# Routed rows added by an indirect gather and an indirect write in place of one-hot products, beside an exchanged front end

## The chip, the cores and the metric

The kernel runs on one core of a Trainium2 chip. A core has five engines with a queue of instructions each: TensorE (PE: matrix products; its weight loads are listed apart as PEld), VectorE (DVE), ScalarE (ACT), GpSimd (POOL) and SyncE (SP), which here only issues transfers. Sixteen DMA engines move data between HBM and the on-chip memories. Transfers can be issued from SP, ACT or GpSimd. The metric is the device time of one execution in microseconds, the median of several runs. The profile is one execution of the same program; its span (116.4 us) is the time between the first and last event of the core and is a little shorter than the device time.

## The reference, cut to what matters

Input x has 2048 tokens of 640 columns. The output is x plus a linear attention block plus a block that routes: it picks the eight tokens with the highest router score, runs them through a gated MLP, and adds the result to these eight rows only.

```python
xn = _layernorm(x)                                   # (1, 2048, 640)

# A: linear attention, 32 heads of 20 columns
q, k, v = split(xn @ wqkv)
phi = lambda t: jnp.where(t > 0, t + 1, jnp.exp(t)) + 1e-6
kv = einsum("bhsd,bhse->bhde", phi(k), v);  z = einsum("bhsd->bhd", phi(k))
A = ((phi(q) @ kv) / (phi(q) . z + 1e-6)) @ wo

# B: eight routed tokens
r = xn @ w_r
idx = argsort(-r)[:, :8]
y = (silu(x_sel @ w_gate) * (x_sel @ w_up)) @ w_down # x_sel: the 8 rows of xn
y = y * sigmoid(r_sel)
B = xn + scatter_add(zero, idx, y)                   # y lands in 8 of 2048 rows

out = x + A + B
```

## The kernel before: the parts that matter

The 2048 tokens are 16 tiles of 128 (T = 16, P = 128); D = 640 and KC = D / P = 5. The program fixes the order on each engine by the order of the calls. It has three stages:

1. For each tile t: layernorm, a transpose of the normalised tile (xnT), the keys K, phi of the keys (PHa on ACT, PHb on DVE), and G, which sums phi(k)-transposed times xn over all tiles.
2. The queries, kv, the folded matrix Mb = kv x wo, the denominators, and the routed MLP, woven together.
3. Output: for each tile phi(q) x Mb, plus the routed rows, plus x + xn, and a store.

Layernorm of one tile goes through small steps:

```python
def ln_a(t):   # statistics of the first 320 columns, DVE (ln_b: the others)
    dve.bn_stats(out=sts[t][:, 0, :], in_=XX[:, t, 1, 0:320])
def ln_g(t):   # mean and variance
    dve.bn_aggr(out=MV[:, t, :], in_=sts[t][:])
def ln_s(t):   # variance + eps on DVE, square root by a power on GpSimd
    dve.tensor_scalar(out=t2[:], in0=MV[:, t, 1:2], scalar1=EPS_BF16, ...)
    pool.tensor_tensor(out=ss[t][:], in0=t2[:], in1=halfc[:], op=ALU.pow)
def ln_c(t, eng):   # c = mean - x, on ACT or DVE
def ln_xn(t, ...):  # SR = 1 / s, xn = -c * SR  -> XX[:, t, 0, :], DVE
```

In the front end before, tiles 0 and 1 are only centred ahead of their transpose (`CT = 2`); the factor 1/sigma goes into the scale of the exponential and the relu. The tiles up to 5 are transposed on TensorE with copies on ACT, those from tile 6 (`TD = 6`) by DMA.

```python
def wk_ld(k0, k1):
    ld(act, wk[:, k0:k1, 0:D], wqkv_v[:, k0:k1, D : 2 * D])
ld(sp, XX[:, 0, 1, :], x_v[:, 0, :])
wk_ld(0, 3)
ld(sp, XX[:, 1, 1, :], x_v[:, 1, :])
wk_ld(3, KC)
ld(sp, XX[:, 2, 1, :], x_v[:, 2, :])
ld(act, wr[:], ...)
act.preload_act_table_set("natural_log_exp_and_others")
# ... cut ...
def PHa(t, hs=(0, 1)):
    kw = {"scale": SR[:, t : t + 1]} if t < CT else {}
    for h in hs:
        act.activation(ek[:, sl], src, AF.Exp, **kw)
        act.activation(rk[:, sl], src, AF.Relu, **kw)
# ... cut ...
stats(0); ln_c0(0, ((0, 3 * P), (3 * P, D))); ln_s(0)
tr_now(0, 0, 5)                 # transpose of the centred tile 0
stats(1); ln_c0(1); ln_s(1); ln_r(0)
K(0, (0, 1), range(0, 2))
tr_now(1, 1, 2)
# ... cut ...
K(0, (0, 1), range(2, KC))
# ... cut: tiles 2 to 5, then the regular loop ...
for t in range(TD, T):
    K(t); PHa(t); rcopy(t)
    # ... PHb(t - 1), ln_xn(t + 2), tr_dma(t + 2), statistics of t + 3 and t + 4 ...
    if t >= 14:
        logit(t - 14, dve)      # router scores of tiles 0 and 1, by DVE
    G(t - 1)
```

The routed rows. `cols[:, 0]` holds the eight token numbers and `cols[:, 1]` their gates, repeated in each group of 32 partitions; `ysb` holds the eight gated MLP rows in the same layout. `onehot()` turns a table of token numbers into OH, which is 1 where a column's token is that of the partition's row. In the output stage a product of OH and ysb starts the sum of every tile, whether or not a routed token lies in it:

```python
def out_sc(ts):                 # two tiles, two halves each: four products
    for t in ts:
        b = obank(t)
        for h in range(2):
            g = 2 * (t % 2) + h
            pe.matmul(PS[:, b + h, 0:HW], lhsT=OH[32 * g : 32 * g + 8, t * P : (t + 1) * P],
                      rhs=ysb[32 * g : 32 * g + 8, h * HW : (h + 1) * HW], start=True, stop=False)
def out_mm(t):                  # ten products of 128 x 320
    for h in range(2):
        for kc in range(KC):
            pe.matmul(PS[:, b + h, 0:HW], lhsT=pqT[:, kc, t * P : (t + 1) * P],
                      rhs=Mb[:, kc, h * HW : (h + 1) * HW], start=False, ...)
def out_ev(t):                  # the last tile goes out in three parts, through DVE and ACT
    dve.tensor_tensor(out=ot, in0=PS[:, b : b + 2, 0:HW], in1=XX[:, t, 1, :], op=ALU.add)
    ld(sp, out_v[:, t, :], ot[:])
# ... cut ...
for t in range(6, T):
    if t % 2 == 0:
        out_sc((t, t + 1))
    out_one(t)                  # out_mm(t), out_ev(t)
```

Three, and from tile 8 on four, pairs of PSUM banks take the output tiles by turns, and four buffers the outgoing rows.

Of the kernel before, what the change touches and what calls it, by code (L numbers as in the profile page):

```python
# [22 lines left out]
CT = 2  # L23
TD = 6
FQ = F // 4
EPS_BF16 = 1.0013580322265625e-05
LOW = S - 1

# [9 lines left out]
def kernel(  # L38
# [62 lines left out]
    def ld(eng, dst, src):  # L101
        eng.dma_start(dst, src)

    def wk_ld(k0, k1):
        ld(act, wk[:, k0:k1, 0:D], wqkv_v[:, k0:k1, D : 2 * D])

    wr = st([KC, P], BF16, "wr")
    wrb = st([P, D], BF16, "wrb", "kv1")
    ld(sp, XX[:, 0, 1, :], x_v[:, 0, :])
    wk_ld(0, 3)  # L110
    ld(sp, XX[:, 1, 1, :], x_v[:, 1, :])
    wk_ld(3, KC)
    ld(sp, XX[:, 2, 1, :], x_v[:, 2, :])
    ld(act, wr[:], B_w_r.rearrange("(kc p) -> kc p", p=P))
    act.preload_act_table_set("natural_log_exp_and_others")
    dve.memset(zero[:], 0.0)
    dve.memset(MVf[:], 0.0)
    ld(sp, XX[:, 3, 1, :], x_v[:, 3, :])


    def warm(n, w=512, b=7):
        for _ in range(n):
            pe.matmul(PS[:, b, 0:w], lhsT=zero[:, 0:P], rhs=zero[:, 0:w], start=True, stop=True)

    warm(9)


# [13 lines left out]

    lg = st([P, CT], F32, "lg")

    def logit(t, eng):
        pr = st([P, D], F32, "pr", "f32a")
        dve.tensor_tensor(out=pr[:], in0=XX[:, t, 0, :], in1=wrb[:], op=ALU.mult)
        if eng is act:
            act.activation(pr[:], pr[:], AF.Identity, accum_out=lg[:, t : t + 1])
        else:
            dve.tensor_reduce(out=lg[:, t : t + 1], in_=pr[:], op=ALU.add, axis=mybir.AxisListType.X)  # L150
# [37 lines left out]
    def ln_r(t):  # L188
        dve.reciprocal(SR[:, t : t + 1], ss[t][:])

    def ln_c0(t, parts=((0, D),)):
        for a, b in parts:
            dve.tensor_scalar(out=XX[:, t, 0, a:b], in0=XX[:, t, 1, a:b], scalar1=MVf[:, t, 0:1], scalar2=None,
                              op0=ALU.subtract)

    def ln_x0(t):
        dve.tensor_scalar(out=XX[:, t, 0, :], in0=XX[:, t, 0, :], scalar1=SR[:, t : t + 1], scalar2=None,
                          op0=ALU.mult)

    def tr_pe(t, lo=(6, HW), hi=(7, 384)):  # L200
        yield from ()
        for (b, o), k0, k1 in ((lo, 0, 3), (hi, 3, KC)):
            pt = PS[:, b, o:512].bitcast(BF16)[:, 0 : (k1 - k0) * P]
            for kc in range(k0, k1):
                pe.transpose(pt[:, (kc - k0) * P : (kc - k0 + 1) * P], XX[:, t, 0, kc * P : (kc + 1) * P], ident[:])
            act.copy(xnT[:, k0:k1, t * P : (t + 1) * P], pt.rearrange("p (k c) -> p k c", c=P))  # L206
            yield

    def tr_now(t, lo, hi):
        for _ in tr_pe(t, (lo, 0), (hi, 0)):  # L210
            pass
# [12 lines left out]
    KB = {1: (3, 4)}  # L224

    def K(t, hs=(0, 1), kcs=range(KC)):
        for kc in kcs:
            for h in hs if len(hs) == 1 or t == 0 else ():
                k_mm(t, h, kc)
        if len(hs) == 2 and t > 0:  # L230
            for h in hs:
                for kc in kcs:
                    k_mm(t, h, kc)

    def k_mm(t, h, kc):
        w = HW + (h if t >= CT else 0)
        pe.matmul(  # L237
            PS[:, KB.get(t, (6, 7))[h], 0:w],
            lhsT=xnT[:, kc, t * P : (t + 1) * P],
            rhs=wk[:, kc, h * HW : h * HW + w],  # L240
            start=(kc == 0),
            stop=(kc == KC - 1),
        )
# [3 lines left out]
    def PHa(t, hs=(0, 1)):  # L247
        if 0 in hs:
            ek = tmp.tile([P, D], BF16, tag="ek", name="ek", bufs=3)
            rk = tmp.tile([P, D], BF16, tag="rk", name="rk", bufs=3)  # L250
            phis[t] = (ek, rk)
        ek, rk = phis[t]
        kw = {"scale": SR[:, t : t + 1]} if t < CT else {}
        for h in hs:
            sl = slice(h * HW, (h + 1) * HW)
            src = PS[:, KB.get(t, (6, 7))[h], 0:HW]
            act.activation(ek[:, sl], src, AF.Exp, **kw)  # L257
            act.activation(rk[:, sl], src, AF.Relu, **kw)  # L258
# [8 lines left out]
    def G(t, aa=range(KC)):  # L267
        for a in aa:
            lhsT = XX[:, t, 0, a * P : (a + 1) * P]
            pe.matmul(  # L270
                PS[:, a, :], lhsT=lhsT, rhs=pk[:, t, 0:512],
                start=(t == 0), stop=(t == T - 1),
            )
            if a < 4:
                pe.matmul(  # L275
                    PS[:, 5, a * P : (a + 1) * P], lhsT=lhsT, rhs=pk[:, t, 512:D],
                    start=(t == 0 and a == 0), stop=(t == T - 1), skip_group_check=True,
                )
# [33 lines left out]
    def hm_copies():  # L312
        for j in range(1, 4):
            ld(sp, hm[32 * j : 32 * j + 32, :], hm[0:32, :])

    def consts_e():
        pool.memset(bm2[0:E2, 0, :], 1.0)
        band(bm2[0:E2, 0, :], P, 8)

# [23 lines left out]
    def consts_d():  # L343
        pool.iota(lowkey[:], pattern=[[-P, T]], base=LOW, channel_multiplier=-1)

    pool_extra = {6: consts_e, 7: consts_b, 8: lambda: (consts_c(), consts_d()), 9: lambda: tok(0, 512),
                  10: lambda: tok(512, 1024), 11: lambda: tok(1024, 1536), 12: lambda: tok(1536, S), 13: consts_g}
# [5 lines left out]
    def loads(t):  # L353
        if t < 5:
            ld(sp, XX[:, 6 + 2 * t : 8 + 2 * t, 1, :], x_v[:, 6 + 2 * t : 8 + 2 * t, :])
        if 8 <= t < 7 + NG:
            g = t - 7
            ld(sp, bm2[32 * g : 32 * g + 32, g, :], bm2[0:E2, 0, :])
        if 7 <= t < 7 + KC:
            ld(sp, wq[:, t - 7, :], wqkv_v[:, t - 7, 0:D])  # L360
        if 12 <= t < 14:
            tr_dma(t - 12)
# [12 lines left out]
    for t in range(0, 5):  # L375
        loads(t)
    sp.dma_start_transpose(xnT[:, 0:4, S - P : S], zero[:])
    ld(sp, wrb[:], B_w_r.unsqueeze(0).to_broadcast([P, D]))
    consts_a()
    hm_copies()  # L380

    def stats(t):
        ln_a(t)
        ln_b(t)
        ln_g(t)

    def stats_b(t):
        ln_b(t)
        ln_g(t)
        ln_s(t)  # L390

    stats(0)
    ln_c0(0, ((0, 3 * P), (3 * P, D)))
    ln_s(0)
    tr_now(0, 0, 5)
    stats(1)
    ln_c0(1)
    ln_s(1)
    ln_r(0)
    K(0, (0, 1), range(0, 2))  # L400
    tr_now(1, 1, 2)
    pe.transpose(PS[:, 5, 256:512].bitcast(BF16)[:, 0:KC], wr[:], ident[0:KC, 0:KC])
    act.copy(wk[:, :, D], PS[:, 5, 256:512].bitcast(BF16)[:, 0:KC])
    K(0, (0, 1), range(2, KC))
    stats(2)
    ln_s(2)
    ln_c(2, dve)
    ln_r(1)
    ln_x0(0)
    ln_xn(2)  # L410
    PHa(0, (0,))
    K(1, (0,))
    tr_now(2, 0, 5)
    PHa(0, (1,))
    K(1, (1,))
    PHa(1)
    ln_a(3)
    stats_b(3)
    ln_c(3, dve)
    ln_a(4)  # L420
    ln_xn(3)
    PHb(0)
    K(2)
    tr_now(3, 1, 2)
    G(0, (0, 3, 4, 1, 2))
    PHa(2)
    rcopy(2)
    ln_x0(1)
    stats_b(4)
    ln_a(5)  # L430
    PHb(1)
    ln_c(4, dve)
    ln_xn(4)
    ln_b(5)
    PHb(2)

    def slot_pe(t):
        K(t)
        PHa(t)
        tr = tr_pe(t + 1)  # L440
        G(t - 2, (0, 1))
        next(tr)
        G(t - 2, (2,))
        next(tr)
        rcopy(t)
        G(t - 2, (3, 4))

    for t in range(3, TD - 1):
        ln_g(t + 2)
        ln_s(t + 2)  # L450
        slot_pe(t)
        ln_c(t + 2, act)
        ln_a(t + 3)
        ln_b(t + 3)
        PHb(t)
        ln_xn(t + 2)
        if t + 2 >= TD:
            tr_dma(t + 2)
    t = TD - 1
    ln_g(t + 2)  # L460
    ln_s(t + 2)
    K(t)
    PHa(t)
    rcopy(t)
    ln_c(t + 2, act)
    ln_a(t + 3)
    ln_b(t + 3)
    PHb(t)
    ln_xn(t + 2)
    tr_dma(t + 2)  # L470
    ln_g(t + 3)
    ln_s(t + 3)
    ln_c(t + 3, dve)
    ln_a(t + 4)
    ln_b(t + 4)
    ln_xn(t + 3)
    tr_dma(t + 3)
    ln_g(t + 4)
    ln_s(t + 4)
    ln_a(t + 5)  # L480
    G(t - 2)
    G(t - 1)

    for t in range(TD, T):
        K(t)
        PHa(t)
        rcopy(t)
        if t == TD:
            ln_c(t + 3, act)
        else:  # L490
            PHb(t - 1)
            if t + 2 < T:
                ln_xn(t + 2)
                tr_dma(t + 2)
            if t + 3 < T:
                stats_b(t + 3)
                ln_c(t + 3, act)
            if t + 4 < T:
                ln_a(t + 4)
        if t >= 14:  # L500
            logit(t - 14, dve)
        G(t - 1)
        if t - 1 in pool_extra:
            pool_extra[t - 1]()
        loads(t)
# [27 lines left out]
    dve.tensor_copy(rbf[:, 0:CT], lg[:])  # L533
# [237 lines left out]
    def out_mm(t):  # L771
        b = obank(t)
        last = t == T - 1
        for h in range(2):
            for kc in range(KC):
                pe.matmul(PS[:, b + h, 0:HW], lhsT=pqT[:, kc, t * P : (t + 1) * P],  # L776
                          rhs=Mb[:, kc, h * HW : (h + 1) * HW],
                          start=False, stop=(kc == KC - 1 and not last))
# [4 lines left out]
    def out_ev(t):  # L783
# [12 lines left out]
        else:  # L796
            dve.tensor_tensor(out=ot[:].rearrange("p (h c) -> p h c", h=2), in0=PS[:, b : b + 2, 0:HW],  # L797
                              in1=XX[:, t, 1, :].rearrange("p (h c) -> p h c", h=2), op=ALU.add)
            ld(sp, out_v[:, t, :], ot[:])

    def out_one(t):
        out_mm(t)
        out_ev(t)
# [90 lines left out]
    out_sc((0, 1))  # L894
# [9 lines left out]
    out_sc((2, 3))  # L904
# [4 lines left out]
    xpx(4)  # L909
    out_one(3)  # L910
    norm(3, 0, 2)
    xpx(5)
    out_sc((4, 5))
# [6 lines left out]
    for t in range(6, T):  # L920
        if t % 2 == 0:
            out_sc((t, t + 1))
        out_one(t)
# [30 lines left out]
```

## Time and profile before

| | before |
|---|---|
| device time, median of 3 | 118.12 us (118.11 to 118.15) |
| span of the profiled execution | 116.4 us |
| granted TensorE clock, mean | 0.995 |
| K products, first to last tile (line 237) | 24.7 us in 160 instructions |
| output products (line 776) | 23.5 us in 160 instructions, 299 ns each |
| one-hot products (line 767) | 32 instructions, 304 ns each |
| evictions of the output (line 797) | 12.4 us in 15 instructions, 824 ns each |
| GpSimd | 23.4 us busy, nothing after 72.6 us |
| moved by DMA | 17.00 MB; 11.96 MB read from HBM, 2.62 MB written |

How to read it: the profile lists busy time of each engine, the granted clock in 40 slices of the span, and groups of instructions by line. The chain of waits is followed back from the last instruction: at each step to what released it, or to the instruction before it on its engine; its pieces add up to the span. A matmul's listed duration overlaps the next one, so the advance of the chain, and not the listed duration, is its cost in a dense stretch. DMA issues give the time from issue to landing.

### The profile page before, as it was taken

The page shows a single profiled execution, that of the slowest core. Times are in us where ns is not written, and L with a number is a line of the kernel's source. Part 1 is how long each engine was busy: PE and PEld are TensorE (multiplying, and loading weights), DVE is VectorE, ACT ScalarE, POOL GpSimd, SP SyncE. Part 2 cuts the span into 40 slices and gives each one's busy share as a digit, 9 for nine tenths or more (in the row PEclk, how much of TensorE's full clock was granted, in tenths as well). Part 3 has the DMA queues.
Part 4 walks back from the last instruction along what each step waited for, and adds up shares of the span by engine and source line. Part 5 has one row for each costly group of instructions (what it writes and reads, how often), then busy time and mean ns, then how long its engine had stood idle before and what let it go on. Part 6 is the DMA issues. An engine that isn't in the chain of part 4 may idle for free.

```text
span 116.4 us, 2659 instructions
## 1 busy us (share of the span) xinstructions
PE 110.2 (95%) x954; PEld 67.8 (58%) x954; DVE 89.2 (77%) x208; ACT 81.8 (70%) x185; POOL 23.4 (20%) x60
## 2 busy tenths in 40 slices
PE   5987899999999999999999999999999999999980
PEld 1454566656666666675575665655556666666650
DVE  2799999899999976985685985779895997555540
ACT  1367999928888886555945878999989699970010
POOL 7432103111569549400000033000000000000000
PEclk9999999999999999999999999999999999999998
DMA  2999700044447676699999990000000313333322
GB/s 78 374 356 361 158 6 0 3 86 86 113 97 85 129 174 114 111 344 348 382 390 406 369 330 19 6 3 0 3 6 0 115 56 118 113 113 113 111 95 76
DMA packets 19943, 17.00 MB, mean 146 GB/s; under 512 B 10234, under 2 KB 18650, under 8 KB 19930
## 3 DMA queue, kind: packets, MB, share of 16 engines
q1 hardware_dynamic: 19072, 15.98, 45.4%
q10 hardware_dynamic: 858, 0.86, 2.2%
q8 instruction: 7, 0.11, 0.4%
q14 instruction: 6, 0.05, 0.1%
HBM read 11.96 MB, written 2.62 MB: 125 GB/s over the span
## 4 chain that ended last, share of the span: by engine, by line
PE 77%; ACT 9%; DMA 6%; DVE 4%; issue 1%; POOL 1%; SPq 0%; ACTq 0%
PE PS L776 19%; PE PS L515 19%; PE PS L237 13%; PE PS L270 10%; DMA XX<-in_A_x_dram 3%; ACT ek L257 3%; DMA xnT<-XX 2%; ACT rk L258 2%; PE PS L275 2%; ACT xnT L206 2%; PE PS L767 2%; PE PS L691 2%; PE PS L697 1%; PE PS L716 1%; ACT c L176 1%
## 5 line engine op out<-in xcount | busy, mean ns | idle before, releaser
L237 PE MATMUL PS<-wk,xnT 128*128 128x320 bf16 (+1 forms) x160 | 24.7, 300 | 0.9 <-ACT rk L258 0.4
L270 PE MATMUL PS<-pk,XX 128*128 128x512 bf16 x80 | 23.7, 379 | 0.1
L515 PE MATMUL PS<-xnT,wq 128*128 128x512 bf16 x100 | 23.7, 380 | 0.0
L776 PE MATMUL PS<-Mb,pqT 128*128 128x320 bf16 x160 | 23.5, 299 | 0.0
L237 PEld LDWEIGHTS <-xnT 128*128 128x128 bf16 x160 | 15.3, 97 | 8.3 <-issue 0.8
L776 PEld LDWEIGHTS <-pqT 128*128 128x128 bf16 x160 | 14.9, 97 | 6.7
L797 DVE TENSOR_TENSOR o<-PS,XX 128x640 bf16<-128x640 f32 x15 | 12.4, 824 | 7.9 <-PE PS L776 7.0
L257 ACT ACTIVATE ek<-PS 128x320 bf16<-128x320 f32 x28 | 12.5, 446 | 8.0 <-PE PS L237 7.9
L521 ACT ACTIVATE qe<-PS 128x512 bf16<-128x512 f32 x20 | 12.2, 610 | 6.6 <-PE PS L515 6.1
L515 PEld LDWEIGHTS <-wq 128*128 128x128 bf16 x100 | 11.2, 118 | 8.1 <-issue 0.3
L572 DVE SCALAR_TENSOR_TENSOR pqT<-qe,qr 128x512 bf16<-128x512 bf16 x20 | 13.4, 681 | 2.0 <-ACT qr L522 2.0
L265 DVE SCALAR_TENSOR_TENSOR pk<-ek,rk 128x640 bf16<-128x640 bf16 x16 | 13.1, 818 | 1.8 <-ACT rk L258 1.5
L275 PE MATMUL PS<-pk,XX 128*128 128x128 bf16 x64 | 14.0, 219 | 0.0
L171 POOL TENSOR_TENSOR s<-t,halfc 128x1 bf16<-128x1 bf16 x16 | 9.0, 561 | 24.9 <-DVE t L170 23.4
L221 ACT ACTIVATE XX<-XX,MR,SR 128x640 bf16<-128x640 bf16 x16 | 13.5, 912 | 0.0
L258 ACT ACTIVATE rk<-PS 128x320 bf16<-128x320 f32 x28 | 12.5, 448 | 0.0
L522 ACT ACTIVATE qr<-PS 128x512 bf16<-128x512 f32 x20 | 12.2, 610 | 0.0
L270 PEld LDWEIGHTS <-XX 128*128 128x128 bf16 x80 | 7.7, 98 | 7.6
L156 DVE BATCH_NORM_STATS2 stats<-XX 128x6 f32<-128x320 bf16 x16 | 7.8, 485 | 1.9 <-DMA XX<-in_A_x_dram 1.9
L176 ACT ACTIVATE c<-XX,MVf 128x640 bf16<-128x640 bf16 x10 | 8.6, 861 | 0.0
L159 DVE BATCH_NORM_STATS2 stats<-XX 128x6 f32<-128x320 bf16 x16 | 7.7, 481 | 0.0
L185 DVE TENSOR_SCALAR XX<-c,SR 128x640 bf16<-128x640 bf16 x14 | 6.0, 430 | 1.6 <-ACT c L176 0.5
(135 smaller groups left out, 128.3 us busy)
## 6 DMA issues: line engine op xcount, KB each, us to landing
out_dram<-o SPq DMA_DIRECT2D x15, 160.0 KB, 1.8
XX<-in_A_x_dram SPq DMA_DIRECT2D x6, 320.0 KB, 5.1
wg<-in_B_w_gate_dram SPq DMA_DIRECT2D x5, 384.0 KB, 6.2
wu<-in_B_w_up_dram SPq DMA_DIRECT2D x5, 384.0 KB, 6.8
wd<-in_B_w_down_dram SPq DMA_DIRECT2D x1, 1920.0 KB
wq<-in_A_wqkv_dram SPq DMA_DIRECT2D x5, 160.0 KB, 2.6
wv<-in_A_wqkv_dram SPq DMA_DIRECT2D x1, 800.0 KB, 5.1
XX<-in_A_x_dram SPq DMA_DIRECT2D x4, 160.0 KB, 4.4
```

What stands on the lines that cost most here:

```text
L221: act.activation(XX[:, t, 1, :], XX[:, t, 1, :], AF.Identity, bias=MR[:, t : t + 1], scale=SR1[:, t : t + 1])
L237: pe.matmul(PS[:, KB.get(t, (6, 7))[h], 0:w], lhsT=xnT[:, kc, t * P : (t + 1) * P], rhs=wk[:, kc, h * HW : h * HW + w], start=(kc == 0), s ...
L257: act.activation(ek[:, sl], src, AF.Exp, **kw)
L258: act.activation(rk[:, sl], src, AF.Relu, **kw)
L265: dve.scalar_tensor_tensor(out=pk[:, t, :], in0=ek[:], scalar=1.0, in1=rk[:], op0=ALU.min, op1=ALU.add)
L270: pe.matmul(PS[:, a, :], lhsT=lhsT, rhs=pk[:, t, 0:512], start=(t == 0), stop=(t == T - 1),)
L275: pe.matmul(PS[:, 5, a * P : (a + 1) * P], lhsT=lhsT, rhs=pk[:, t, 512:D], start=(t == 0 and a == 0), stop=(t == T - 1), skip_group_check= ...
L515: pe.matmul(PS[:, bank, :], lhsT=by5(wq[:, kc, :])[:, m, :], rhs=xnT[:, kc, tb * TBLK : (tb + 1) * TBLK], start=(kc == 0), stop=(kc == KC ...
L521: act.activation(e, PS[:, bank, :], AF.Exp)
L572: dve.scalar_tensor_tensor(out=pqT[:, m, tb * TBLK : (tb + 1) * TBLK], in0=e, scalar=1.0, in1=r, op0=ALU.min, op1=ALU.add,)
L776: pe.matmul(PS[:, b + h, 0:HW], lhsT=pqT[:, kc, t * P : (t + 1) * P], rhs=Mb[:, kc, h * HW : (h + 1) * HW], start=False, stop=(kc == KC - ...
L797: dve.tensor_tensor(out=ot[:].rearrange("p (h c) -> p h c", h=2), in0=PS[:, b : b + 2, 0:HW], in1=XX[:, t, 1, :].rearrange("p (h c) -> p h ...
```

## The change

It does two things. In the output stage, the tiles 0 to 9 (`TF = 10`) get no one-hot products. They are stored without the routed rows; later GpSimd gathers the routed rows that lie in these tiles from the output in HBM, DVE adds the MLP rows, and GpSimd writes them back. Token numbers of 1280 and over are out of bounds and are dropped; they are served by the one-hot products of tiles 10 to 15, which stay. The purpose is to take work from TensorE.

```diff
+TF = 10
-                          start=False, stop=(kc == KC - 1 and not last))
+                          start=(t < TF and kc == 0), stop=(kc == KC - 1 and not last))
+    idxu = st([C, 1], I32, "idxu")
+    og = st([C, D], BF16, "og", "hl")
+    low_rows = out[0][0 : TF * P, :]
+    def fix_init():
+        dve.memset(og[:], 0.0)
+        dve.tensor_copy(idxu[:], cols[0:C, 0:1])
+    def fix_gather():
+        pool.indirect_dma_start(
+            out=og[:], out_offset=None, in_=low_rows,
+            in_offset=bass.IndirectOffsetOnAxis(ap=idxu[:, 0:1], axis=0),
+            bounds_check=TF * P - 1, oob_is_err=False)
+    def fix_add():
+        dve.tensor_tensor(out=og[:], in0=og[:], in1=ysb[0:C, :], op=ALU.add)
+        pool.indirect_dma_start(
+            out=low_rows, out_offset=bass.IndirectOffsetOnAxis(ap=idxu[:, 0:1], axis=0),
+            in_=og[:], in_offset=None, bounds_check=TF * P - 1, oob_is_err=False)
     ... cut: out_sc((0, 1)), out_sc((2, 3)), out_sc((4, 5)) go; fix_init() stands before out_one(3) ...
     for t in range(6, T):
-        if t % 2 == 0:
+        if t % 2 == 0 and t >= TF:
             out_sc((t, t + 1))
+        if t == TF + 3:
+            fix_gather()
+        if t == T - 2:
+            fix_add()
         out_one(t)
```

And it exchanges the front end: no tile is only centred. All are normalised before the transpose, tiles 0 to 3 are transposed on TensorE and the others by DMA, loads and constants are issued in another order, and the router scores of all tiles come from the 641st column of K.

```diff
-    ld(sp, XX[:, 0, 1, :], x_v[:, 0, :])
-    wk_ld(0, 3)
-    ld(sp, XX[:, 1, 1, :], x_v[:, 1, :])
-    wk_ld(3, KC)
-    ld(sp, XX[:, 2, 1, :], x_v[:, 2, :])
-    ld(act, wr[:], ...)
-    act.preload_act_table_set(...)
+    ld(sp, XX[:, 0, 1, :], x_v[:, 0, :])
+    act.preload_act_table_set(...)
+    ld(act, wr[:], ...)
+    ld(act, XX[:, 1, 1, :], x_v[:, 1, :])
+    ld(sp, wk[:, :, 0:HW], wqkv_v[:, :, D : D + HW])
+    ld(sp, XX[:, 2, 1, :], x_v[:, 2, :])
+    ld(sp, wk[:, :, HW:D], wqkv_v[:, :, D + HW : 2 * D])
     ... cut ...
     def hm_copies():
         for j in range(1, 4):
-            ld(sp, hm[32 * j : 32 * j + 32, :], hm[0:32, :])
+            ld(act, hm[32 * j : 32 * j + 32, :], hm[0:32, :])
     ... cut: ten warming products in place of nine, single ones of 256 columns between the first tiles ...
+    ln_a(0); ln_b(0); ln_g(0); ln_s(0); ln_c(0, dve); ln_a(1)
+    ln_xn(0, ((0, 3 * P), (3 * P, D)))
+    tr_pe(0, 0, act, act)
+    ln_b(1); ln_g(1); ln_a(2); ln_s(1); ln_c(1, act)
+    K(0, (0,), 4)
+    PHa(0, (0,), 4)
+    ln_b(2); ln_xn(1)
+    tr_pe(1, 2, act, act)
+    ln_g(2); ln_a(3); ln_s(2); ln_c(2, dve)
+    K(0, (1,), 4); PHa(0, (1,), 4); rcopy(0, 5); K(1, (0,))
+    ln_b(3); ln_xn(2); PHa(1, (0,)); tr_pe(2, 0, act, act)
+    ln_g(3); ln_a(4); ln_s(3); ln_c(3, dve)
+    K(1, (1,)); PHa(1, (1,)); rcopy(1); K(2, (0,))
+    hm_copies()
+    ln_b(4); ln_xn(3); ln_g(4); PHb(0); ln_s(4); tr_pe(3, 3, act, act)
     ... cut: K 2, tiles 4 and 5, G 0, K 3, G 1, G 2 ...
-    for t in range(TD, T):
+    for t in range(4, T):
         K(t)
     ... cut ...
-        if t >= 14:
-            logit(t - 14, dve)
```

## The prediction

> **What bounds the kernel now.** I read the page's engine rows and clock row first, then the table of stretches, then the chain of waits in order of time, then the timeline of the last stretch, and the DMA issues last.
>
> ```profile
> PE 110.2 (95%) x954; PEld 67.8 (58%) x954; DVE 89.2 (77%) x208; ACT 81.8 (70%) x185; POOL 23.4 (20%) x60
> ...
> 24.83:51.50 26.67, 26.67 (x190) 16.86 (x191) 23.54 (x60) 19.88 (x57) 14.10 (x34) 1.00 0.60 127
> 51.50:87.40 35.90, 35.90 (x402) 21.78 (x402) 27.38 (x58) 28.79 (x61) 2.02 (x8) 1.00 0.54 193
> 87.40:113.05 25.65, 25.64 (x219) 16.52 (x218) 17.43 (x23) 15.59 (x22) 0.00 (x0) 1.00 0.25 90
> ```
>
> The first row is busy time by engine; the others are stretches with their length, then the busy time of PE, PEld, DVE, ACT and POOL, the granted clock, the DMA share and GB/s. From 24.83 us on TensorE is busy in every microsecond at full clock, while VectorE has 17.43 of 25.65 us in the last stretch. What TensorE is spared after 24.83 us is saved one for one. Before that the chain runs through other engines:
>
> ```profile
> 1.28 3.97 DMA XX<-in_A_x_dram
> 5.27 0.49 DVE stats L156
> ...
> 8.02 0.17 DVE t L170
> ...
> 8.26 0.63 POOL s L171
> 8.91 0.17 DVE SR L183
> ...
> 22.18 2.60 DMA xnT<-XX
> 24.83 1.54 PE PS L237 x10
> ...
> 100.46 0.25 PE PS L767 x4
> 100.71 2.83 PE PS L776 x20
> 103.54 0.25 PE PS L767 x4
> ```
>
> Columns are start and length. At the front the landing of x tile 1 (5.27 us), the statistics, the GpSimd power and the scalar engine's evictions set the pace. At the end it is a strict beat of 2.83 us for two output tiles (L776) and 0.25 us for their four one-hot products (L767): 3.08 us a pair.
>
> ```profile
> 103.63 0.82 DVE L797 TENSOR_TENSOR o<-PS,XX 128x640 bf16<-128x640 f32 x1 [0.54 <-PE PS L776]
> ...
> 109.78 0.82 DVE L797 TENSOR_TENSOR o<-PS,XX 128x640 bf16<-128x640 f32 x1 [0.54 <-PE PS L776]
> ...
> 111.50 0.82 DVE L797 TENSOR_TENSOR o<-PS,XX 128x640 bf16<-128x640 f32 x1 [0.89 <-PE PS L776]
> ...
> 113.40 0.33 DVE L793 CAST o<-PS 128x160 bf16<-128x160 f32 x1 [0.65 <-ACT o L792]
> ```
>
> These are the evictions of tiles 9, 13, 14 and the last part of 15. VectorE idles 0.54 and 0.89 us by turns: there is a hole of 0.9 us between tiles 13 and 14, where the new add will stand.
>
> ```profile
> out_dram<-o SPq DMA_DIRECT2D x15, 160.0 KB, 1.8
> ...
> hm<-hm SPq DMA_DIRECT2D x3, 40.0 KB, 3.6
> out_dram<-o SPq DMA_DIRECT2D x1, 80.0 KB, 1.6
> ...
> out_dram<-o SPq DMA_DIRECT2D x1, 40.0 KB, 1.5
> ```
>
> An ordinary store lands 1.5 to 1.8 us after its issue.
>
> **What the Trainium skill says.** (1) "TensorE: Matmul & The Clock Gate", Part 3 on packing small matmuls: products that use different row groups of the array run at the same time. The trace agrees: one one-hot product takes 304 ns, four of them advance the chain by 0.25 us. (2) "DMA: Bandwidth & Descriptors", section on the anatomy of one DMA on the GpSimd path: about 2.0 us fixed, mostly the write receipt; its specifications give about 1 us to the first byte on this path against 0.6 on the hardware path. The kernel before has no DMA from GpSimd, so no trace here shows it; its stores at 1.5 to 1.8 us fit the size of the receipt. (3) The same page, "Two DMAs through the same engine are not ordered": only the completion semaphore orders a read after a write. So the gather has to wait for the stores of tiles 0 to 9, and does in the built program: it waits for tile 9's store and not for tile 10's. (4) "GPSIMD Engine Reference", Instruction dispatch: the first call of freshly loaded GpSimd code costs about 6 us. No run here shows whether an indirect transfer is such a call.
>
> **The change part by part.**
>
> *One-hot products removed.* Tiles 0 to 9 lose five groups of four. Each group is 0.25 us on the chain, all after 24.83 us: 5 x 0.25 = -1.25 us. Nothing else sets in there: without them a pair needs 2.83 us of TensorE, against 2 x 0.82 = 1.64 us of eviction and two scalings of about 0.82 us on ACT, and the normalisations that tiles 4 to 15 need were done 2 us or more ahead.
>
> *Gather.* Tile 9's eviction ends at 103.63 + 0.82 = 104.45; its store lands 1.8 us later, about 106.3 (all on the clock of before; the saving shifts all of it alike). First byte 1 us and 2.0 us fixed give an estimate, from the skill's page, of 3.0 us: og is there at about 109.3. The add is wanted when tile 13's eviction leaves VectorE, at about 110.55. Slack 1.2 us.
>
> *Add.* The normalisation moves 1280 bf16 columns in 0.81 us, so 640 take about 0.4 us: 110.55 to 110.95, in front of tile 14's eviction at 111.50. It fits the hole. Clearing og and the index cast, about 0.25 us together, fall where VectorE has slack. Cost 0.
>
> *Indirect write.* Issued at about 111.0, again an estimated 3.0 us: 114.0. The last ordinary store is issued at about 113.75 and lands 1.5 us later, 115.25. Hidden by 1.2 us. For the chance that one of the three new steps is slower than this I add 0.25 us.
>
> *The front end, which is exchanged too.* In place of centring tiles 0 and 1, transposing, and applying 1/sigma in the exponential's scale, all tiles are normalised before the transpose; tiles 4 and 5 go through DMA transposes and not TensorE; wk comes in column halves on SP; x tile 1 is issued on ACT behind the table load (1.28 us) and the wr load (0.62); the three hm copies move from SP to ACT's queue; the two DVE logits go. I walk the new order with durations of this trace: pair of statistics 0.91, aggregate 0.25, from t to the reciprocal by way of GpSimd 0.89 (8.02 to 8.91), reciprocal to end of xn 0.6, two copies of transposes on ACT 0.75, half of a K 0.68, exponential and relu of a half without scale 0.66 (with it 0.84), PHb 0.73.
> - x tile 1: 0.8 + 1.28 + 0.62 = 2.7, plus 2.4 that x tile 0 took to land: 5.2 us, as now. If the queue runs on past the table load, 4.4.
> - The order has tile 1's first statistics ahead of tile 0's xn: 5.2 + 0.4 + 0.2, then xn in two parts; transposes at 6.05, first copy done 6.9, first K at 6.95 (6.17 before). K 0 half 0 ends at 7.7.
> - Tile 1: t at 7.4, reciprocal 8.3, xn ends 8.9, transposes to 9.3, copies to 10.05. Tile 2: xn ends 10.9. Tile 3: t at 11.5, xn ends 13.0. PHb of tile 0 at 13.15 to 13.9.
> - TensorE: K 2's second half ends 14.1, and G 0 follows without a wait. From 14.1 up to K 6 it has five G of about 1.3 and three K of 1.37, 10.75 us: 24.85, if nothing waits. Before starts K 6 at 24.83. DMA transposes land 2.6 us after xn: tile 4 at 18.3 for 19.5, tile 5 at 21.1 for 22.2.
> - But the hm copies took 1.90 us to issue on SP (three at 0.63). On ACT they start with the second half of PHa 1, at 12.4, and end at 14.3, where the copies of tile 3 would have begun at 13.4. That puts K 3 back by 0.4 to 0.9 us; I take 0.55. K 6 starts at 25.4.
> The front costs +0.55 us, and I trust this to about 0.9 either way.
>
> Sum: 118.12 - 1.25 + 0.55 + 0.25 = 117.67, say 117.6 us.
>
> **The rivals.** *The gather comes late and stalls VectorE.* Its slack is 1.2 us to the free slot and 1.6 us before tile 14's eviction moves. For it: descriptors made in software from indices in SBUF have no measured time here; if point (4) applied, it would be some 6 us. Against: GpSimd has been idle since 72.6 us, and nothing else loads the DMA queues then. A 5 us gather lands at 111.3, moves the write to 114.7: time still about 117.8. With 9 us the last two evictions start after 115, and the result is about 121.5. *The write outlives the last store.* It has 1.2 us; at 5 us in place of 3.0 it ends at 116.0 and costs 0.8 us: 118.4. *The front decides.* If the older front is really worse than in my walk, by a DMA transpose that arrives late or a chain through the GpSimd power at each of tiles 1 to 3, K 6 starts at 26.5 and the result is 118.7; if x tile 1 comes at 4.4 and the hm issues are swallowed, it starts at 24.2 and the result is 116.4. *TensorE is not the bound once the products go*: then the gain is smaller than 1.25; the 0.54 and 0.89 us of idle VectorE in each pair speak against it.
>
> **Range and chances.** The front gives 0.9 us either way, the tail 0 to +1 us with a thin branch of +3 to +4. That gives 116.5 to 118.9 as the range for 8 in 10. Faster by over 2% is below 115.76 us and needs a front a whole microsecond better than now beside a hidden tail: 0.04. Slower by over 2% is above 120.48 and needs the late gather: 0.07. Within 2%: 0.89.
>
> **What would show it.** In the chain after, pairs of tiles up to tile 9 follow each other at 2.83 us and groups of one-hot products appear three times only; K 6 starts between 24.3 and 26.3 us, with the cause of any gap before it in ACT's copies of tile 3 or in a DMA transpose; the gather is released by tile 9's store; the wait of the add for the gather is near zero; the write lands before the last store. I am wrong if VectorE stands still ahead of the add, if the end of the span follows the GpSimd DMA, or if TensorE is dense much later than 25.4 us.

## The result and the profile after

| | before | after |
|---|---|---|
| device time, median | 118.14 us (118.11 to 118.25, 4 runs) | 116.91 us (116.42 to 117.13, 4 runs) |
| ratio to before, 95% interval | | 0.9888 (0.9857 to 0.9920) |
| span of the profiled execution | 116.4 us | 115.4 us |
| start of K of tile 6 | 24.83 us | 25.36 us |
| output stage, first product to last | 87.47 to 113.05: 25.58 us | 87.99 to 111.91: 23.92 us |

117.6 us was predicted, within a range of 116.5 to 118.9. The change is 1.2 us faster, where the prediction had 0.5. The page and the table of stretches of after (length, then busy time of PE, PEld, DVE, ACT and POOL, granted clock, DMA share, GB/s):

```profile
PE 108.2 (94%) x931; PEld 67.1 (58%) x931; DVE 85.2 (74%) x204; ACT 81.2 (70%) x185; POOL 25.1 (22%) x62
...
q0 software_dynamic: 64, 0.01, 0.1%
```

```profile
25.36:52.04 26.68, 26.68 (x191) 16.86 (x190) 19.82 (x54) 20.32 (x58) 10.54 (x25) 1.00 0.58 136
52.04:87.99 35.95, 35.95 (x404) 22.03 (x403) 27.27 (x57) 28.85 (x61) 1.86 (x8) 1.00 0.49 174
87.99:111.90 23.91, 23.91 (x198) 16.12 (x196) 17.87 (x26) 15.52 (x22) 2.08 (x2) 1.00 0.27 98
```

The queue q0 is new: the two GpSimd transfers. TensorE still works without a gap from the start of K 6 to the end. The two middle stretches are as long as before, within 0.1 us, so the whole difference lies ahead of 25.36 us (0.53 us lost in this execution) and behind 87.99 us (1.66 us gained).

The chain of waits of after (start, length):

```profile
1.47 4.41 DMA XX<-in_A_x_dram
5.90 0.49 DVE stats L141
...
12.63 0.57 ACTq L101
...
16.02 1.56 PE PS L200 x10
...
87.99 2.72 PE PS L706 x20
...
92.86 9.53 PE PS L706 x70
102.39 0.25 PE PS L697 x4
102.64 2.83 PE PS L706 x20
```

Seventy output products without a one-hot block take 9.53 us, 0.136 each, so twenty take 2.72. Where a block stands ahead of them, the same twenty are booked at 2.83; the seventy run straight into a block (102.39) and show no such addition. That 0.11 us belongs to the block, though the chain lists it under the ordinary products behind it. At the front, x tile 1 lands at 5.9 us, and ACT's queue issues the hm copies (ACTq) before it gets to tile 3.

The timeline of the end, and the two transfers' issues with their time to landing:

```profile
106.43 1.18 POOL L741 DMA_INDIRECT og<-out_dram,idxu  x1 [32.98 <-DVE o L727]
...
108.64 0.82 DVE L727 TENSOR_TENSOR o<-PS,XX 128x640 bf16<-128x640 f32 x1 [0.54 <-PE PS L706]
...
109.39 0.47 DVE L748 TENSOR_TENSOR og<-og,ysb 8x640 bf16<-8x640 bf16 x1
110.18 0.90 POOL L749 DMA_INDIRECT out_dram<-og,idxu  x1 [2.58 <-DVE og L748]
110.36 0.82 DVE L727 TENSOR_TENSOR o<-PS,XX 128x640 bf16<-128x640 f32 x1 [0.50 <-issue]
```

```profile
og<-out_dram,idxu POOLq DMA_INDIRECT x1, 2.5
out_dram<-og,idxu POOLq DMA_INDIRECT x1, 2.0
```

The add starts in the very moment in which VectorE has done tile 13 (109.39), and 0.50 us of the hole before tile 14 is left over. The gather landed at 106.43 + 2.5 = 108.9, so it had 0.5 us to spare. The write landed at 110.18 + 2.0 = 112.2; the last store is issued about 112.6 and needs 1.5 us. Nothing of the three steps shows in the time.

### The profile page after: what moved, and what is told of

The parts are those of the page before. It is cut to its first block, busy times and chain, and to the rows that moved or that the text cites. A ratio compares the mean times of both kernels' runs of the same rounds, so it can differ in the third digit from the quotient of the medians.

```text
span 115.4 us, 2622 instructions
## 1 busy us (share of the span) xinstructions
PE 108.2 (94%) x931; PEld 67.1 (58%) x931; DVE 85.2 (74%) x204; ACT 81.2 (70%) x185; POOL 25.1 (22%) x62
## 4 chain that ended last, share of the span: by engine, by line
PE 85%; ACT 4%; DMA 4%; DVE 1%; ACTq 1%; issue 1%
PE PS L706 19%; PE PS L446 19%; PE PS L200 17%; PE PS L231 14%; DMA XX<-in_A_x_dram 4%; PE PS L236 3%; PE PS L621 2%; PE PS L627 2%; PE PS L646 1%; ACT xnT L181 1%; PE PS L601 1%; ACT rk L219 1%; PE PS L512 1%; ACTq L101 1%; ACT ek L218 1%; PE PS L253 1%
## 5 line engine op out<-in xcount | busy, mean ns | idle before, releaser
L706 PE MATMUL PS<-Mb,pqT 128*128 128x320 bf16 x160 | 22.9, 299 | 0.0
L218 ACT ACTIVATE ek<-PS 128x320 bf16<-128x320 f32 x32 | 14.4, 449 | 7.9 <-PE PS L200 7.8
L219 ACT ACTIVATE rk<-PS 128x320 bf16<-128x320 f32 x32 | 14.5, 453 | 0.0
L156 POOL TENSOR_TENSOR s<-t,halfc 128x1 bf16<-128x1 bf16 x16 | 9.6, 597 | 22.1 <-DVE t L155 22.0
L161 ACT ACTIVATE c<-XX,MVf 128x640 bf16<-128x640 bf16 x12 | 10.4, 866 | 0.1
L741 POOL DMA_INDIRECT og<-out_dram,idxu x1 | 1.2, 1175 | 33.0 <-DVE o L727 33.0
```

Source lines behind the costliest of these rows:

```text
L218: act.activation(ek[:, sl], PS[:, b + h, 0:HW], AF.Exp)
L219: act.activation(rk[:, sl], PS[:, b + h, 0:HW], AF.Relu)
```

## The experiments

| run | what it is | ratio to before (95%) | x tile 1's statistics, K of tile 6 start at |
|---|---|---|---|
| after | the change | 0.9888 (0.9857 to 0.9920) | 5.90, 25.36 |
| after again | the same once more | 0.9842 (0.9829 to 0.9856) | 5.37, 24.84 |
| tail only | old front, new output stage | 0.9859 (0.9842 to 0.9877) | 5.52, 25.08 |
| front only | new front, old output stage | 0.9990 (0.9975 to 1.0005) | 5.44, 24.90 |
| no fix | after without gather, add, write | 0.9863 (0.9845 to 0.9881) | 5.94, 25.87 |
| hm on SP | after, hm copies back on SP | 0.9855 (0.9836 to 0.9874) | 5.42, 24.77 |
| double | before, each block twice | 1.0126 (1.0104 to 1.0148) | 5.30, 24.87 |
| split | before, blocks of two products | 1.0218 (1.0203 to 1.0234) | 5.55, 25.12 |
| late fix | old front, twelve tiles, late add | 0.9950 (0.9934 to 0.9966) | 5.45, 25.00 |
| accumulate | old front, twelve tiles, one adding write | 0.9828 (0.9814 to 0.9841) | 5.48, 25.04 |
| x1 first | hm on SP and an earlier load of x tile 1 | 0.9832 (0.9820 to 0.9845) | 4.89, 24.69 |
| combined | x1 first and accumulate | 0.9815 (0.9802 to 0.9828) | 5.16, 24.81 |

My theory after the result: a block of one-hot products costs TensorE 0.36 us and not 0.25, the three steps at the end cost nothing, and the front costs about what I had said. The rival: the blocks cost 0.25 us, and the rest of the gain is the front's.

### The tail alone

```diff
 (kernel before, front end unchanged)
-    out_sc((0, 1)) ... out_sc((4, 5))
-        if t % 2 == 0:
+        if t % 2 == 0 and t >= TF:             # TF = 10; fix_init, fix_gather, fix_add as in after
             out_sc((t, t + 1))
```

> The front end of before with the output stage of after. If a block of four one-hot products costs 0.36 us of TensorE (0.25 of its own and 0.11 that the chain books on the products before it), five blocks are worth 1.8 us: 116.3 us, ratio to before 0.985. If a block costs only the 0.25 us that I predicted with, and the rest of the gain comes from the exchanged front end, 116.9 us, ratio 0.989. The output stage, from its first product to its last, 23.9 us in the first case against 24.4 in the second.

Measured 116.70 against 118.36 us, -1.67 us (1.46 to 1.87 by the interval); 1.25 us would be a ratio of 0.9894 and lies outside. The chain of this run:

```profile
87.72 2.72 PE PS L777 x20
...
92.60 9.53 PE PS L777 x70
```

The output stage lasts from 87.72 to 111.65, 23.93 us, as in after. The whole gain is here. The 0.11 us stands on the other side of the block than the expectation has it: on the products behind it, not before it.

### The front alone

```diff
 (kernel after)
-    start=(t < TF and kc == 0)
+    start=False                                 # one-hot products for all tiles, no gather, add, write
```

> The front end of after with one-hot products for all 16 tiles and no gather. If the older front costs what the two traces show (first product of K of tile 6 at 25.36 in place of 24.83 us, output stage 0.59 us later), 118.7 us, ratio 1.005, and together with the run of the tail alone the two shares add up to after. If the front is neutral and the tail gained only 1.25 us, 118.1 us, ratio 1.000.

118.16 against 118.36 us: ratio 0.9990 (0.9975 to 1.0005). The theory fell here: the front costs nothing, where both the prediction and my reading of after's trace had +0.5. The table above shows why that reading misled. K of tile 6 starts 19.46 us after the first statistics of x tile 1 in after, after again and front only, and 19.56 us after them in before and tail only. The new order is 0.1 us shorter. The statistics of x tile 1 start anywhere from 5.27 to 5.55 us in the six profiles with the old front, and from 5.37 to 5.94 in the five in which the new front issues the tile behind the table load; after's profiled execution had a late one.

### Without the three steps

```diff
 (kernel after)
-    fix_init()
-        if t == TF + 3:
-            fix_gather()
-        if t == T - 2:
-            fix_add()
```

The routed rows of tiles 0 to 9 are left out of the output here.

> After without clearing og, gather, add and indirect write: the routed rows of tiles 0 to 9 are left out of the output. If these are wholly hidden, 116.9 us as after, within 0.2. If they cost something at the end or by the hole on VectorE, up to 0.5 us less.

116.64 us, ratio 0.9863, against 0.9842 for after again and 0.9888 for after: not faster than the one, and within the intervals of the other. The steps are hidden, as far as some 0.3 us can be told apart. In this run's profile the distance from x tile 1 to K 6 is 19.93 us, because the first products on TensorE were slow: five of K 0 took 1.33 us where after has 0.85.

### The hm copies back on SP

```diff
-            ld(act, hm[32 * j : 32 * j + 32, :], hm[0:32, :])
+            ld(sp, hm[32 * j : 32 * j + 32, :], hm[0:32, :])
```

> After with the three hm copies issued on SP again. In the trace of after ACT issues them from 12.63 to 14.50 us and the copies of tile 3's transposes start at 14.54 us. If that issue is what holds up K of tile 3, the run gains 0.4 to 0.6 us: 116.4 us. If the late landing of x tile 1 (5.9 us) sets the front, nothing changes: 116.9 us.

116.54 us, ratio 0.9855: no gain over after again (0.9842). K of tile 3 does start sooner (15.15 for 16.02 us in after; x tile 1 explains 0.48 of it). But the next wait takes over, in this run's chain:

```profile
15.18 4.20 DMA xnT<-XX
19.42 1.54 PE PS L200 x10
```

The DMA transpose of tile 4 lands 4.2 us after its issue, not 2.6, and K of tile 4 waits for it. In after the same transpose, issued at 15.65 us, took 2.6. K 6 comes 19.35 us after the statistics of x tile 1 here and 19.46 in after: of the 0.39 us gained at K 3, 0.1 is left.

### What a block costs: doubled and split

```diff
 double (the routed rows are added twice):
     out_sc((t, t + 1))
+    out_sc((t, t + 1), first=False)
 split:
-    if t % 2 == 0:
-        out_sc((t, t + 1))
-    out_one(t)
+    out_sc((t,))
+    out_one(t)
```

> Before with each block of four one-hot products issued twice in a row (the routed rows are added twice). If a block's cost is 0.25 us of its own products plus one fixed 0.1 us for the change from full products to row-packed ones, the second half of a doubled block costs about 0.25 or less: 8 x 0.25 = +2.0 us at most, 120.3 us. If every four products cost the full 0.36 us, +2.8 us, 121.1 us.

> Before with the same 32 one-hot products in 16 blocks of two, one block ahead of each tile. If the change between full and row-packed products costs a fixed part at each block, eight more blocks cost 8 x 0.1 us or more: 119.1 us or above. If only the number of products counts, 118.3 us, no change.

Doubled: 119.87 against 118.50 us, +1.26% (1.04 to 1.48), 1.5 us for 32 more products (1.1 of them in the output stage of the trace, 26.67 us for 25.58; the spans of all its executions are longer by the same 1.1, so the rest lies outside them). Split: 121.06 us, +2.18% (2.03 to 2.34), 2.6 us for not one product more. The chains of doubled and split:

```profile
97.96 0.38 PE PS L767 x8
98.34 2.83 PE PS L776 x20
```

```profile
98.62 0.24 PE PS L767 x2
98.86 1.47 PE PS L776 x10
```

A pair of tiles takes 0.38 + 2.83 = 3.21 us with a block of eight, 3.08 with four, 2.72 with none: 0.49, 0.36, 0. A tile with a block of two takes 0.24 + 1.47 = 1.71 us against 1.36: 0.35. So two products in a block cost as much as four, and four more only 0.13 us. Some 0.2 us of each block are fixed. The trace shows them at the turns from full-array products to row-packed ones and back; a block of after, with its weight loads (PEld):

```profile
105.40 0.10 PEld L697 LDWEIGHTS <-tokrow 8*128 8x128 bf16 x4 [0.27 <-issue]
105.41 0.31 PE L697 MATMUL PS<-ysb,tokrow 8*128 8x320 bf16 x4
...
105.65 2.57 PEld L706 LDWEIGHTS <-pqT 128*128 128x128 bf16 x20
105.65 2.90 PE L706 MATMUL PS<-Mb,pqT 128*128 128x320 bf16 x20
```

Between full products the starts lie 0.136 us apart, and the weights of each are loaded 0.13 us ahead of it. At both turns the load starts only with its product. In before, the block of 100.39 us starts 0.23 us after the start of the full product ahead of it, and the next full product 0.24 us after the block: 0.1 us more than the usual beat each time. The chain has the first of these inside the 0.25 us of the block, the second in the 0.11 us behind it. In doubled, the second four are loaded 0.13 us ahead again. That the exposed weight load (0.10 us) is the reason for each 0.1 us fits these traces; no run tests it by itself.

### After once more, and adding in flight

```diff
 accumulate (old front, TF = 12; replaces gather, add and write, issued ahead of tile 15)
+    pool.indirect_dma_start(out=low_rows, out_offset=IndirectOffsetOnAxis(ap=idxu[:, 0:1], axis=0),
+        in_=ysb[0:C, :], in_offset=None, bounds_check=TF * P - 1, oob_is_err=False, compute_op=ALU.add)
```

> After once more, as the measure for the other runs. If tail (0.986) and front (0.999) add up, ratio to before 0.985, 116.5 us; if the first measurement stands and the two do not add up, 0.989, 116.9 us.

> Front end of before; tiles 0 to 11 without one-hot products, and in place of gather, add and write one indirect write that adds to the rows in HBM, released by the store of tile 11. Six blocks at 0.36 us: 2.1 us off before, 116.2 us, if the one transfer lands before the last store (released near 107.6 us, 3.5 us as the gather took: 111.1, against 113.5). If adding in flight takes over 6 us, the end follows it and the time is 117 us or more.

After again: 116.60 against 118.50 us, 0.9842. The shares add up: 0.9859 x 0.9990 = 0.985, inside this interval and just below that of the first measurement. Why after took 116.91 us the first time and 116.60 the second is shown only in part: of the first four executions one has a profile, with its late x tile 1. Accumulate: 116.38 us, 0.9828. Its output stage lasts from 87.67 to 111.24, 23.57 us, 0.36 less than the tail alone for one block less. The issue of the adding write:

```profile
out_dram<-ysb,idxu POOLq DMA_INDIRECT x1, 2.9
```

It starts at 108.72 us and lands at 111.6, ahead of the last store (113.5).

### The steps made late

```diff
 (tail alone, TF = 12)
+        if t == T - 1:
+            fix_gather()
         out_one(t)
+    fix_add()                                   # after the last eviction
```

> Front end of before; tiles 0 to 11 without one-hot products, gather released by the store of tile 11, the add after the last eviction on VectorE. TensorE is spared six blocks, 116.3 us if the three steps stayed hidden. But the gather lands near 111.1 us, the add ends at 112.5, and the indirect write lands 2.3 us later, 114.8, against 113.5 for the last ordinary store: the end is put back by about 1.3 us, 117.5 us, ratio 0.992, and the end of the span follows the GpSimd transfer.

117.76 against 118.39 us, ratio 0.9950. TensorE's work is the same as in accumulate, the time 1.2% more. The end of this run's timeline:

```profile
111.91 0.32 DVE L794 CAST o<-PS 128x160 bf16<-128x160 f32 x1 [0.65 <-ACT o L793]
112.15 0.47 DVE L818 TENSOR_TENSOR og<-og,ysb 8x640 bf16<-8x640 bf16 x1
112.95 0.90 POOL L819 DMA_INDIRECT out_dram<-og,idxu  x1 [2.68 <-DVE og L818]
```

The write lands at 112.95 + 2.0 = 114.95, 1.2 us or so after the last store (113.8). This is the rival "the write outlives the last store", made true: it costs its overhang in full.

### x tile 1 sooner, and both together

```diff
 (kernel after, hm copies on SP)
+    ld(act, XX[:, 1, 1, :], x_v[:, 1, :])
     act.preload_act_table_set(...)
     ld(act, wr[:], ...)
-    ld(act, XX[:, 1, 1, :], x_v[:, 1, :])
```

> After with x tile 1 as the first load of ACT's queue (ahead of the table load and wr) and the hm copies on SP. In all traces so far the start of K of tile 6 follows the landing of x tile 1 at a fixed distance (19.5 us in the new order, 19.6 in the old). Issued 0.65 us sooner it should land 0.3 to 0.6 us sooner and shift all by as much: 116.1 us. If another wait takes its place (the DMA transpose of tile 4 did, when hm alone was moved), 116.5 us.

> The front end of the run with x tile 1 first, and the output stage of the run that adds in flight (tiles 0 to 11 without one-hot products). If the shares add up, 0.3 us below the run that adds in flight: 116.0 us, ratio 0.980. If the front ends are equal, 116.3 us.

x1 first: 116.47 us, 0.9832. The tile's statistics start at 4.89 us, 0.5 sooner than in after again, but K 6 only 0.15 sooner. The chain of this run again goes through the transpose of tile 4:

```profile
14.81 4.49 DMA xnT<-XX
```

In all three runs with the new front and the hm copies on SP this transpose is late (4.20, 4.49 and in combined 4.35 us); in the four with the copies on ACT (after, after again, front only, no fix) it took 2.6. It is not late as a whole: the trace has sixteen reports of its landing, of which fifteen came 2.4 to 2.6 us after the issue in every one of the seven runs. In x1 first TensorE waits 0.43 us for it ahead of K 4, most of what the earlier landing gave; x tile 1 first with the copies on ACT was not run.

Combined: 116.19 us, 0.9815 (0.9802 to 0.9828), the fastest of all. It beats before by 2.2 us and after again by about 0.3 us; against accumulate alone (0.9828) the intervals overlap.

## Why the prediction was right, point by point

*What bounds the kernel.* Right. TensorE is dense from K 6 on, and what it is spared there comes off the time one for one.

*One-hot products, -1.25 us.* The mechanism was right and the size too small: -1.67 us (tail alone). The term that was mis-sized is the cost of a block, taken as the 0.25 us that the chain lists under the one-hot line. It is 0.353 us between full products (3.076 a pair, the mean of five, less 2.723). Four of the five blocks stood so; the second followed other packed products (L582) and cost 0.25. That makes 4 x 0.353 + 0.25 = 1.66, the 1.66 us of the traces. The view before already held it:

```profile
92.95 1.36 PE PS L776 x10
```

Ten output products with no block just ahead of them took 1.36 us, so twenty need 2.72 and not the 2.83 that I read as their own. The section of "TensorE: Matmul & The Clock Gate" on packing that I used says that the four run together, which the traces bear out (two cost the same as four).

*The front, +0.55 us.* Wrong: -0.1 us (-0.3 to +0.06, front alone). Single steps seemed to hold: G 0 at 14.32 us (14.1 predicted), hm issues from 12.63 to 14.50 (12.4 to 14.3), K 6 at 25.36 (25.4). That was luck. These times stood on x tile 1 at 5.2 us and it came at 5.9: counted from its landing, the walk was 0.7 us too long (20.2 us to K 6, measured 19.46). About 0.5 of this had gathered in the layernorms of tiles 1 to 3: xn of tile 3 ends 7.3 us after the landing, not 7.8. The term for the hm copies was too large as well: of the 0.55 charged, 0.1 is left at K 6 when they are moved (hm on SP), where tile 4's late transpose takes over. Two sums were 0.1 us too high besides: 2.7 + 2.4 is 5.1, and five G and three K make 10.6. On the landing itself both my cases missed. ACT's queue did run past the table load (x tile 1 is issued at 1.47 us), and still it took 4.4 us to land among the other loads, where I had counted 2.4.

*Gather, add, write: 0, and +0.25 us for a slow one.* The steps were right, the allowance was not needed. From the last of GpSimd's semaphore waits (105.4 us; tile 9's store had landed at 105.1) to the gather's landing took 3.5 us, the estimate from "DMA: Bandwidth & Descriptors" was 3.0; from the end of the add (109.86) to the write's landing 2.3. The gather's slack was 0.5 us and not 1.2. The 6 us that "GPSIMD Engine Reference" gives under Instruction dispatch for the first call of fresh GpSimd code did not occur: the gather's listed start came 1.0 us after those waits, the write's 0.3 after the add. Only five of the eight token numbers lay in the tiles 0 to 9: the trace of after has ten packets of 1280 bytes on q0, five for each transfer. With more rows nothing was measured but the six of the twelve-tile runs.

*The rivals.* A late gather did not happen. The outliving write did not happen here and costs its overhang where it is forced. "The front decides" did not happen: K 6 started at 25.36 and 24.84 us, between the 24.2 and 26.5 of its two cases. "TensorE is not the bound once the products go" is out: seventy products ran without a gap.

*The sum.* 118.12 - 1.67 - 0.1 = 116.3, against 116.91 and 116.60 measured. All three terms erred in the same direction, by 0.4, 0.65 and 0.25 us. The range held the result since the front was given 0.9 us either way; 116.60 lies 0.1 us above its lower end.

What stays open: why one part of tile 4's transpose is late when the hm copies go ahead of it on SP, and what makes x tile 1 land anywhere from 5.4 to 5.9 us in one and the same kernel. No run tests either.

## What to carry to other kernels

Price a group of instructions by the length of a stretch with it and without it, not by its own rows: here the chain booked 0.11 of a block's 0.36 us on the products behind it. A front end whose first data wander by half a microsecond is compared by distances from their landing, over several executions. Work that only a few rows need can leave the busiest engine for an indirect write on an idle one, as long as its last transfer lands before the last ordinary store does (here the write landed 2.3 us after the add, and the adding write 4 us after the store that it waited for).

## What the runs showed of the hardware

- Turning between full-array and row-packed products costs about 0.2 us per block (blocks of two, four and eight: 0.35, 0.36, 0.49 us), 0.1 at each turn, where a weight load of 0.10 us starts only with its product.
- An indirect transfer by GpSimd with eight token numbers, of which five are in bounds (rows of 1280 bytes): 2.5 us from listed start to landing as a gather from HBM, 2.0 us as a write; with six in bounds 2.9 us as a write that adds in flight.
- ACT's queue issues loads while its table load of 1.28 us runs; but loads among ACT's instructions hold up the ones behind: three issues from 12.63 to 14.50 us, and the waiting copy started at 14.54.
- A DMA transpose of a 128 x 640 tile lands 2.6 us after issue by the median; tile 4's, the first of the new order, landed after 4.2 to 4.5 us in the three runs that issued three small copies ahead of it on the same queue (SP), and after 2.6 us in the four that issued them on ACT. The first one of the kernel before (tile 6, at 22.18 us) took 2.6.
- TensorE's first products can run slowly at a granted clock of 1.00: five of 128x320 in 1.33 us for 0.85, seen in one execution (no fix).
